# Attention and MLP on one core: the first v tile on ScalarE's DMA queue, the last stores split differently, score units one piece earlier

## The chip, the cores and the metric

The kernel runs on one core of one Trainium2 chip. The metric is the device time of one execution in microseconds (us). The profile's span, from the first to the last instruction, is 1.7 to 1.9 us shorter than that time. Each run of a kernel gave one execution with a full profile and, where it was timed, five more beside executions of the kernel before.

## The reference

```python
def _attn_ref(q, k, v, s):            # q, k, v: (8, 8, 576, 64); s: (8, 8, 576)
    scores = scale * np.matmul(q, k.transpose(0, 1, 3, 2))
    causal = np.triu(np.ones((S, S), dtype=bool), k=1)
    cum = np.cumsum(np.maximum(s, 0.0), axis=-1)
    bias = -(cum[:, :, :, None] - cum[:, :, None, :])
    scores = np.where(causal, -1000000000.0, scores + np.minimum(bias, 0.0))
    ...                               # softmax over the last axis
    return np.matmul(attn, v)

def _moe_ref(x, w_in, w_out):         # x: (4608, 512); w_in: (512, 2048); w_out: (2048, 512)
    h = x @ w_in
    return gelu_erf(h) @ w_out        # written out with erf in the original
```

The output is float32, 4608 by 512.

## The kernel before

The kernel computes attention batch by batch, and weaves the attention of batch c+1 into the MLP of token chunk c, so that TensorE always has matmuls to do. The bias is separable, so v is scaled by a weight `wb` that comes from the running sum of s. The parts that matter here are the loads, the first attention items, and the stores (cuts are marked with `# ...`).

```python
LAST = (NCH - 1, 2)           # subtiles from here on are stored after the branch
# ...
def load_v(b, eng, sts=range(ST)):             # one DMA of 256 KB for each 128 rows of v
    t = raws[b, "v"] if (b, "v") in raws else raw_v(b)
    for st in sts:
        n_st = 128 if st < ST - 1 else SL
        eng.dma_start(out=t[:n_st, st, :, :], in_=bass.AP(tensor=v.tensor,
            offset=v.offset + b * H * S * D + st * 128 * D,
            ap=[[D, n_st], [S * D, H], [1, D]]))      # source in runs of 64 floats = 256 B

s_sw = const.tile([64, S], fp32, name="s_sw")
nc.sync.dma_start(out=s_sw, in_=s.flatten_outer_dims())
for g in range(HG):
    for i in range(2):
        load_qk(0, i, g, 1)                    # GpSimd: float32 in memory, bf16 on chip
# ...
exp_set(); filler(17); cum_sum(); masks(); weights()
# ...
load_v(0, nc.gpsimd, (0, 1))
load_w(0, 0); load_w(0, 1); load_w(0, 2)       # w_in in four parts, w_out in four parts
scale_v(0, 1, nc.gpsimd)
# ... all further loads, on GpSimd
tr_qk(0, 0, 0); tr_qk(0, 1, 0)                 # 32x32 transposes by VectorE
sc_first(0, 0)                                 # scores and exponentials
tr_qk(0, 0, 1); tr_qk(0, 1, 1)
sc_first(0, 1, (0,)); filler(1); sc_first(1, 0, (0,))
mk_item(0, 0, 0)                               # mask
scale_v(0, 0)                                  # vv = v * wb, by VectorE
sc_first(1, 0, (1,), 0)
av_item(0, 0, 0)                               # P @ vv, the first reader of it
# ...
def l2_item(c, subs, f0=0, f1=FT, store=True):
    # ... matmuls into y_of[c, sub]
    if f1 == FT and store:
        for sub in subs:
            o_sb = ost.tile([128, KO * 128], fp32, tag="osb", bufs=3, name="o_sb")
            if c == 0: nc.scalar.activation(o_sb, y_of[c, sub], func=AF.Copy)
            else:      nc.vector.tensor_copy(o_sb, y_of[c, sub])
            nc.sync.dma_start(out=out[r0 : r0 + 128, :], in_=o_sb)
# ...
rv = nc.values_load(bad[0:1, 0:1], min_val=0, max_val=1)
with tc.If(rv > 0):                            # a general path, not taken with these inputs
    # ...
for sub in range(LAST[1], 4):                  # after the branch
    o_sb = ost.tile([128, KO * 128], fp32, tag="osb", bufs=3, name="o_sb")
    # scalar_copy stands for ScalarE's activation with Copy
    for i, (copy, eng) in enumerate([(nc.vector.tensor_copy, nc.sync), (scalar_copy, nc.scalar)]):
        cols = slice(i * 256, i * 256 + 256)
        copy(o_sb[:, cols], y[:, cols])
        eng.dma_start(out=out[r0 : r0 + 128, cols], in_=o_sb[:, cols])
```

Of the kernel before, what the change touches and what calls it, by code (L numbers as in the profile page):

```python
# [19 lines left out]
def kernel(  # L20
# [10 lines left out]
    nc = tc.nc  # L31
    fp32 = mybir.dt.float32
    bf16 = mybir.dt.bfloat16
    AF = mybir.ActivationFunctionType
# [17 lines left out]
    NCH = n_tok // NB  # L52
# [17 lines left out]
    ITS = [(0, 1), (2, 3, 4)]  # L70


    LAST = (NCH - 1, 2)

    EPS = 2.0 ** -17
    MAX_SC = 3.0
# [41 lines left out]
    def load_v(b, eng, sts=range(ST)):  # L118
# [3 lines that stand above are left out]
            eng.dma_start(  # L122
                out=t[:n_st, st, :, :],
                in_=bass.AP(
                    tensor=v.tensor,
                    offset=v.offset + b * H * S * D + st * 128 * D,
                    ap=[[D, n_st], [S * D, H], [1, D]],
                ),
            )

    s_sw = const.tile([64, S], fp32, name="s_sw")
    nc.sync.dma_start(out=s_sw, in_=s.flatten_outer_dims())
    for g in range(HG):
        for i in range(2):
            load_qk(0, i, g, 1)
# [4 lines left out]
    def load_w(which, i):  # L140
# [16 lines left out]
        out=uptri, in_=uptri, compare_op=ALU.is_gt, fill=1.0, base=0, pattern=[[-1, 128]],  # L157
# [322 lines left out]
    def l2_item(c, subs, f0=0, f1=FT, store=True):  # L480
        gT = gT_of[c]
        if f0 == 0:
            for sub in subs:
                y_of[c, sub] = yps.tile([128, KO * 128], fp32, tag="mlp", bufs=2, name="o_ps")
        for ft in range(f0, f1):
            for sub in subs:
                nc.tensor.matmul(  # L487
                    y_of[c, sub], lhsT=gT[:, ft, sub * 128 : (sub + 1) * 128], rhs=w_out_r[:, ft, :],
                    start=(ft == 0), stop=(ft == FT - 1),
                )  # L490
        if f1 == FT and store:
            for sub in subs:
                o_sb = ost.tile([128, KO * 128], fp32, tag="osb", bufs=3, name="o_sb")
                if c == 0:
                    nc.scalar.activation(o_sb, y_of[c, sub], func=AF.Copy)
                else:
                    nc.vector.tensor_copy(o_sb, y_of[c, sub])  # L497
                r0 = c * NB + sub * 128
                nc.sync.dma_start(out=out[r0 : r0 + 128, :], in_=o_sb)

    def exp_set():
        nc.scalar.preload_act_table_set("natural_log_exp_and_others")  # L502
# [18 lines left out]
    nc.scalar.activation(vv[0][:, :, :, D], wb[:, :, 0:H], func=AF.Copy)  # L521
    filler(3)
    filler(3, raws[0, "qk"][:, 1, 0, :128])
    load_v(0, nc.gpsimd, (0, 1))
    load_w(0, 0)
    load_w(0, 1)
    load_w(0, 2)
# [10 lines left out]
    load_v(1, nc.gpsimd, (2, 3, 4))  # L538
    tr_qk(0, 0, 0)
    tr_qk(0, 1, 0)  # L540
    sc_first(0, 0)
    tr_qk(0, 0, 1)
    tr_qk(0, 1, 1)
# [1 line left out]
    filler(1)  # L545
    sc_first(1, 0, (0,))
    mk_item(0, 0, 0)
    scale_v(0, 0)
    sc_first(1, 0, (1,), 0)
    av_item(0, 0, 0)  # L550
    mk_item(0, 1, 0, 0, 2)
# [15 lines left out]
    sc, mk, av = sc_item, mk_item, av_item  # L567
# [5 lines left out]
    for c in range(NCH):  # L573
        b = c + 1
        if c > 0 and b + 1 < B:
            load_qks(b + 1)
            load_v(b + 1, nc.gpsimd)
        if c == 0:

            late = [  # L580
                [], [], [], [], [(av, 0, 0, 2), (av, 0, 1, 2)],
                [(av, 0, 0, 3), (av, 0, 1, 3)], [(to_xT, 0, 2, True), (to_xT, 0, 3, True)],
                [], [(scale_v, 0, 4), (av, 0, 0, 4)], [(av, 0, 1, 4)], [(to_xT, 0, 4, True)],
            ] + [[]] * 5
            for half in range(2):
                for f2 in range(FT // 2):
                    l1_item(0, f2, half * 256, half * 256 + 256)
                    for f, *a in late[8 * half + f2]:
                        f(*a)
                    if f2 % 2 and 3 <= 8 * half + f2 <= 11:  # L590
                        square_v(0, 4 * half + f2 // 2 - 1)
        else:
            for f2 in range(FT // 2):
                l1_item(c, f2)
                for g, it in late_of.get(c, [])[f2 : f2 + 1]:
                    av(c, g, it)
                if b < B and f2 < HG:
                    tr_qk(b, 0, f2)
                    tr_qk(b, 1, f2)
                if b < B and f2 == 2:  # L600
                    den_col(b)
                    for st in range(2):
                        scale_v(b, st)
                if b < B and f2 == 3:
                    for st in range(2, ST):
                        scale_v(b, st)
                if b < B and 4 <= f2 < 4 + HG:
                    absmax(b, f2 - 4)
                if c == 2 and f2 == 7:
                    cert_decay()  # L610
                if f2 < ST and c < B:
                    square_v(c, f2)
        if b < B:
            if c == 0:
                for g in range(HG):
                    for i in range(2):
                        tr_qk(b, i, g)
                den_col(b)
            exp_set()
            if c == 0:  # L620
                load_qks(2)
                load_v(2, nc.gpsimd)
                side = [[] for _ in range(16)]
                side[0] = [(sc, b, 0, 0), (scale_v, b, 0), (scale_v, b, 1), (mk, b, 0, 0)]
                side[3] = [(sc, b, 1, 0), (mk, b, 1, 0)]
                side[5] = [(sc, b, 0, 1), (av, b, 0, 0), (av, b, 0, 1)]
                side[6] = [(av, b, 1, 0, True), (av, b, 1, 1, True), (scale_v, b, 2), (mk, b, 0, 1)]
                side[7] = [(to_xT, b, 0, True), (sc, b, 1, 1)]
                side[8] = [(to_xT, b, 1, True), (scale_v, b, 3), (av, b, 0, 2), (gelu_set,), (mk, b, 1, 1)]
                side[9] = [(av, b, 0, 3)]  # L630
                side[11] = [(av, b, 1, 2, True), (scale_v, b, 4), (square_qk, 0, 0, 0), (square_qk, 0, 0, 1)]
                side[12] = [(av, b, 1, 3, True), (square_qk, 0, 1, 0), (square_qk, 0, 1, 1)]
                side[13] = [(to_xT, b, 2, True)]
                side[14] = [(to_xT, b, 3, True)]
                groups(c, (0, 1), side[:8])
                for sub in (2, 3):
                    groups(c, (sub,), side[4 * sub : 4 * sub + 4])
            else:

                side = [[] for _ in range(16)]  # L640
                sc_at = (1, 4, 6, 8) if b < 4 else (2, 5, 8, 11)
                for at, (g, u) in zip(sc_at, [(0, 0), (1, 0), (0, 1), (1, 1)]):
                    side[at].append((sc, b, g, u))
                side[sc_at[3]].append((gelu_set,))
                mk_at = (4, 6, 8, 10) if b < 4 else (5, 8, 11, 14)
                for at, (g, u) in zip(mk_at, [(0, 0), (1, 0), (0, 1), (1, 1)]):
                    side[at].append((mk, b, g, u))
                av_at = (5, 6, 8, 9) if b < 4 else (6, 7, 9, 10)
                for at, (g, it) in zip(av_at, [(0, 0), (0, 1), (1, 0), (1, 1)]):
                    side[at].append((av, b, g, it))  # L650
                if b < 4:
                    side[10].append((av, b, 0, 2))
                    side[11].append((av, b, 1, 2))

                    side[15].extend([(av, b, 0, 3), (av, b, 1, 3)])
                if c == 1:
                    side[0].append((absmax, c, 0))
                    side[12].extend([(square_qk, c, 1, 0), (square_qk, c, 1, 1)])
                    side[3].append((cert_exp,))
                for sub in range(4):  # L660
                    groups(c, (sub,), side[4 * sub : 4 * sub + 4])
        else:
            for sub in range(4):
                l2_item(c, (sub,), store=(c, sub) < LAST)
                if c == B - 1:
                    (cert_1, cert_2, cert_3, cert_4)[sub]()
# [3 lines left out]
    with tc.If(rv > 0):  # L670
        with tc.tile_pool(name="gen", bufs=1) as gen, tc.tile_pool(
# [5 lines left out]
            a, step = 0, 1  # L677
# [120 lines left out]
    with tc.manual_schedule():  # L798
        for sub in range(LAST[1], 4):
            y = y_of[LAST[0], sub]  # L800
            r0 = LAST[0] * NB + sub * 128
            o_sb = ost.tile([128, KO * 128], fp32, tag="osb", bufs=3, name="o_sb")
            for i, (copy, eng) in enumerate(
                [(nc.vector.tensor_copy, nc.sync), (lambda o, a: nc.scalar.activation(o, a, func=AF.Copy), nc.scalar)]  # L804
            ):
                cols = slice(i * 256, i * 256 + 256)
                copy(o_sb[:, cols], y[:, cols])  # L807
                eng.dma_start(out=out[r0 : r0 + 128, cols], in_=o_sb[:, cols])  # L808


# [28 lines left out]
```

## Time and profile before

| before | |
|---|---|
| time, median of 3 (range) | 315.05 us (314.75 to 315.15) |
| span of the profiled execution | 312.2 us |
| TensorE busy | 300.7 us, 96% |
| VectorE, ScalarE, GpSimd busy | 63%, 62%, 17% |
| last matmul's end, and from there to the end of the span | 306.7 us, 5.5 us |

A share of busy time says little about a change like this. What counts is where TensorE, which does almost all of the work, stands still: those few places are at the start, where transfers have not landed, and after its last matmul. The prediction shows the lines.

### The profile page before, as it was taken

Reading aid. Unit: us, or ns where it says so; the run is one execution under the profiler, and the core shown is the slowest. Engines: PE = TensorE matmul, PEld = TensorE weight load, DVE = VectorE, ACT = ScalarE, POOL = GpSimd, SP = SyncE. Lnnn points to the kernel's source line nnn. Section 1 sums busy time; section 2 is a strip of 40 time slices with the busy share of each in tenths; the row PEclk is TensorE's granted clock in tenths of the full one; section 3 lists DMA queues with packets and bytes.
Section 4 is the critical chain, followed back from the end, with each engine's and each line's share of the span. In section 5 each row is a group of like instructions: output and inputs, shape, how many; then the busy total and the mean of one; then the engine's idle time right before and its main releaser. Section 6 shows DMA issues by size and latency. Waiting matters only on the chain. (4 is left out here: it accounts for less than half of the span.)

```text
span 312.2 us, 6053 instructions
## 1 busy us (share of the span) xinstructions
PE 300.7 (96%) x2466; PEld 154.9 (50%) x2506; DVE 195.7 (63%) x397; ACT 193.5 (62%) x263; POOL 54.3 (17%) x73
## 2 busy tenths in 40 slices
PE   8999999999999999999999999999999999999992
PEld 3577655444554455445454545444544454444441
DVE  8866767797779685955697559845994531350010
ACT  3876878878848763865686558665875677006300
POOL 8473340151003300150006000500000000000000
PEclk9999999999999999999999999999999999999999
DMA  7999999969541963097219940822110311020012
GB/s 137 222 230 210 224 212 278 188 150 204 158 68 44 211 161 103 8 207 181 86 35 174 206 103 18 169 78 75 45 27 34 103 53 25 37 93 7 1 73 70
DMA packets 32211, 36.73 MB, mean 118 GB/s; under 512 B 16752, under 2 KB 21360, under 8 KB 32176
## 3 DMA queue, kind: packets, MB, share of 16 engines
q0 software_dynamic: 11552, 23.07, 37.8%
q1 hardware_dynamic: 20336, 12.93, 15.2%
q8 instruction: 21, 0.34, 0.5%
q10 hardware_dynamic: 288, 0.26, 0.2%
q14 instruction: 14, 0.11, 0.1%
HBM read 36.85 MB, written 9.44 MB: 148 GB/s over the span
## 5 line engine op out<-in xcount | busy, mean ns | idle before, releaser
L487 PE MATMUL o_ps<-w_out_r,gT 128*128 128x512 bf16 x551 | 131.9, 380 | 2.7 <-issue 1.6
L471 PE MATMUL h_ps<-xT,w_in_r 128*128 128x512 bf16 (+1 forms) x625 | 131.1, 357 | 1.7 <-DVE xT L417 0.6
L476 ACT ACTIVATE gT<-h_ps 128x1024 bf16<-128x1024 f32 (+1 forms) x80 | 75.0, 938 | 63.7 <-PE h_ps L471 62.6
L471 PEld LDWEIGHTS <-w_in_r 128*128 128x128 bf16 x640 | 59.8, 98 | 55.4 <-issue 1.2
L487 PEld LDWEIGHTS <-gT 128*128 128x128 bf16 x576 | 52.1, 98 | 57.4 <-issue 3.3
L363 ACT ACTIVATE P<-sc_ps 128x1024 bf16<-128x1024 f32 x56 | 54.3, 1021 | 28.8 <-PE sc_ps L348 28.8
L122 POOL DMA_DIRECT2D raw_v<-in_v_dram x40 | 34.0, 862 | 125.8 <-ACT sq L215 115.4
L497 DVE COPY o_sb<-o_ps 128x512 f32<-128x512 f32 x30 | 20.7, 691 | 49.3 <-PE o_ps L487 49.3
L187 DVE STREAM_TRANSPOSE qkT<-raw_qk 128x576 f32<-128x576 f32 x32 | 37.2, 1238 | 0.2 <-DMA raw_qk<-in_k_dram 0.2
L448 DVE RECIPROCAL rc<-av 128x4 f32<-128x4 f32 (+1 forms) x80 | 14.0, 175 | 35.2 <-PE av L439 35.1
L449 DVE TENSOR_TENSOR x<-av,rc 128x256 bf16<-128x256 f32 (+1 forms) x80 | 33.8, 423 | 2.9
L439 PEld LDWEIGHTS <-P 128*128 128x128 bf16 x576 | 26.8, 98 | 16.0 <-DVE x L449 0.9
L207 DVE TENSOR_REDUCE amx<-raw_qk 128x2 f32<-128x2304 bf16 x13 | 32.7, 2535 | 0.0
L439 PE MATMUL av<-vv,P 128*128 128x65 bf16 x576 | 30.4, 194 | 0.4 <-DVE x L449 0.2
L223 DVE TENSOR_TENSOR vv<-raw_v,wb 128x512 bf16<-128x512 f32 (+1 forms) x39 | 25.3, 692 | 4.3 <-DMA raw_v<-in_v_dram 4.3
L371 DVE TENSOR_TENSOR P<-P,tri_bf 128x1024 bf16<-128x1024 bf16 (+1 forms) x33 | 22.1, 672 | 8.5 <-ACT P L363 8.4
L215 ACT ACTIVATE sq<-raw_v 128x512 bf16<-128x512 f32 (+1 forms) x40 | 24.8, 621 | 0.0
L348 PE MATMUL sc_ps<-qkT 32*128 32x256 bf16 (+2 forms) x560 | 18.0, 250 | 0.0
L348 PEld LDWEIGHTS <-qkT 32*128 32x128 bf16 x560 | 11.7, 92 | 12.2 <-issue 9.3
L502 ACT ACT_TABLE_LOAD x8 | 10.3, 1283 | 0.9 <-PEq L823 0.7
L505 ACT ACT_TABLE_LOAD x8 | 10.3, 1283 | 0.1
L804 ACT ACTIVATE o_sb<-o_ps 128x256 f32<-128x256 f32 x2 | 0.8, 383 | 14.3 <-DVE o_sb L807 13.8
(81 smaller groups left out, 100.2 us busy)
## 6 DMA issues: line engine op xcount, KB each, us to landing
out_dram<-o_sb SPq DMA_DIRECT2D x34, 256.0 KB, 2.2
raw_v<-in_v_dram POOLq DMA_DIRECT2D x32, 256.0 KB, 5.5
raw_qk<-in_q_dram POOLq DMA_DIRECT2D x7, 576.0 KB, 7.5
raw_qk<-in_k_dram POOLq DMA_DIRECT2D x7, 576.0 KB, 10.8
w_in_r<-in_moe_w_in_dram POOLq DMA_DIRECT2D x4, 512.0 KB, 9.8
w_out_r<-in_moe_w_out_dram POOLq DMA_DIRECT2D x4, 512.0 KB, 15.1
raw_v<-in_v_dram POOLq DMA_DIRECT2D x8, 128.0 KB, 6.1
raw_qk<-in_q_dram POOLq DMA_DIRECT2D x2, 288.0 KB, 5.2
```

The lines of the kernel that those rows point to most:

```text
L122: eng.dma_start(out=t[:n_st, st, :, :], in_=bass.AP(tensor=v.tensor, offset=v.offset + b * H * S * D + st * 128 * D, ap=[[D, n_st], [S * D ...
L187: nc.vector.transpose(qkT[b % 2][:, i, g, :S, :].rearrange("p s e -> p (s e)").bitcast(fp32) .rearrange("p (l j) -> p j l", j=LT), raws[b, ...
L207: nc.vector.tensor_reduce(amx[:, b * HG + g], raws[b, "qk"][:, :, g, :], axis=AX, op=ALU.max, apply_absolute_value=True,)
L215: nc.scalar.activation(sq[:n_st], raws[b, "v"][:n_st, st].rearrange("p h d -> p (h d)"), func=AF.Square, accum_out=sumv[:n_st, b, st : st ...
L223: eng.tensor_tensor(vv[b % 2][:n_st, st, :, 0:D], raws[b, "v"][:n_st, st, :, :], w.unsqueeze(2).to_broadcast([n_st, H, D]), op=MULT,)
L348: nc.tensor.matmul(s_ps[h // 2][:, h % 2, off : off + n], lhsT=qk[r, 1, g, jt * 128 : jt * 128 + 128, e], rhs=qk[r, 0, g, i0 : i0 + n, e], ...
L363: nc.scalar.activation(P[:, 2 * h2 : 2 * h2 + 2, o : o + 512], s_ps[h2], func=AF.Exp, scale=scale)
L439: nc.tensor.matmul(o_ps[:, h, :], lhsT=P[:, h, off : off + 128], rhs=vv[b % 2][:, jt, 4 * g + h, :], start=(i == 0), stop=(i == len(BLK[it ...
L449: nc.vector.tensor_tensor(x_of[b, it][:n, g * 256 : g * 256 + 256].rearrange("p (h d) -> p h d", d=D), o_ps[:n, :, 0:D], rc[:n].unsqueeze( ...
L471: nc.tensor.matmul(h_ps[:, i, :], lhsT=w_in_r[:, ko, ft * 128 : (ft + 1) * 128], rhs=xT[:, ko, c * NB + n0 : c * NB + n1], start=(ko == 0) ...
L476: nc.scalar.activation(gT_of[c][:, f2 * 2 : f2 * 2 + 2, n0:n1], h_ps, func=AF.Gelu)
L487: nc.tensor.matmul(y_of[c, sub], lhsT=gT[:, ft, sub * 128 : (sub + 1) * 128], rhs=w_out_r[:, ft, :], start=(ft == 0), stop=(ft == FT - 1),)
```

## The change

The intent is to shorten both ends. The first v tile goes out on ScalarE's idle queue as its first act, so that its scaling can be done in a gap between VectorE's transposes. The last subtile but one is stored before the branch. Some attention items move by a piece. (A subtile is 128 of a chunk's 512 tokens. A piece is one of the 16 parts into which a chunk's second MLP layer is cut; attention items stand between them. A score unit computes a block of scores and their exponentials.)

```diff
-    LAST = (NCH - 1, 2)
+    LAST = (NCH - 1, 3)
     nc.sync.dma_start(out=s_sw, in_=s.flatten_outer_dims())
+    load_v(0, nc.scalar, (0,))
-    load_v(0, nc.gpsimd, (0, 1))
+    load_v(0, nc.gpsimd, (1,))
     tr_qk(0, 1, 0)
+    scale_v(0, 0)
     sc_first(0, 0)
     mk_item(0, 0, 0)
-    scale_v(0, 0)
 # ... l2_item
-                if c == 0:
+                eng = nc.scalar if (c, sub + 1) == LAST else nc.sync
+                if c == 0 or eng is nc.scalar:
-                nc.sync.dma_start(out=out[r0 : r0 + 128, :], in_=o_sb)
+                eng.dma_start(out=out[r0 : r0 + 128, :], in_=o_sb)
 # ... chunk 0: batch 0's last block transposed in the second layer, not in the first
-                [], [(scale_v, 0, 4), (av, 0, 0, 4)], [(av, 0, 1, 4)], [(to_xT, 0, 4, True)],
+                [], [(scale_v, 0, 4), (av, 0, 0, 4)], [(av, 0, 1, 4)],
-                side[3] = [(sc, b, 1, 0), (mk, b, 1, 0)]
+                side[3] = [(sc, b, 1, 0), (to_xT, 0, 4, True), (mk, b, 1, 0)]
 # ... batches 4 to 7: scores, masks and value products one piece earlier
-                sc_at = (1, 4, 6, 8) if b < 4 else (2, 5, 8, 11)
+                sc_at = (1, 4, 6, 8) if b < 4 else (1, 4, 7, 10)
 # ... (mk_at and av_at likewise)
 # ... after the branch
-            for i, (copy, eng) in enumerate([(nc.vector.tensor_copy, nc.sync), (scalar_copy, nc.scalar)]):
+            for i in range(2):
-                copy(o_sb[:, cols], y[:, cols])
-                eng.dma_start(out=out[r0 : r0 + 128, cols], in_=o_sb[:, cols])
+                nc.vector.tensor_copy(o_sb[:, cols], y[:, cols])
+                nc.sync.dma_start(out=out[r0 : r0 + 128, cols], in_=o_sb[:, cols])
```

Below, "start part" is the first v tile and its scaling, "middle part" the later transposition with the score units, "end part" the stores.

More of the change, by code (lines that the diff above doesn't have):

```diff
@@ L582 @@
                 [(av, 0, 0, 3), (av, 0, 1, 3)], [(to_xT, 0, 2, True), (to_xT, 0, 3, True)],
-                [], [(scale_v, 0, 4), (av, 0, 0, 4)], [(av, 0, 1, 4)], [(to_xT, 0, 4, True)],
-            ] + [[]] * 5
+                [], [(scale_v, 0, 4), (av, 0, 0, 4)], [(av, 0, 1, 4)],
+            ] + [[]] * 6
             for half in range(2):
@@ L644 @@
                 side[sc_at[3]].append((gelu_set,))
-                mk_at = (4, 6, 8, 10) if b < 4 else (5, 8, 11, 14)
+                mk_at = (4, 6, 8, 10) if b < 4 else (4, 7, 10, 13)
                 for at, (g, u) in zip(mk_at, [(0, 0), (1, 0), (0, 1), (1, 1)]):
                     side[at].append((mk, b, g, u))
-                av_at = (5, 6, 8, 9) if b < 4 else (6, 7, 9, 10)
-                for at, (g, it) in zip(av_at, [(0, 0), (0, 1), (1, 0), (1, 1)]):
+                for at, (g, it) in zip((5, 6, 8, 9), [(0, 0), (0, 1), (1, 0), (1, 1)]):
                     side[at].append((av, b, g, it))
@@ L802 @@
             o_sb = ost.tile([128, KO * 128], fp32, tag="osb", bufs=3, name="o_sb")
-            for i, (copy, eng) in enumerate(
-                [(nc.vector.tensor_copy, nc.sync), (lambda o, a: nc.scalar.activation(o, a, func=AF.Copy), nc.scalar)]
-            ):
+            for i in range(2):
                 cols = slice(i * 256, i * 256 + 256)
-                copy(o_sb[:, cols], y[:, cols])
-                eng.dma_start(out=out[r0 : r0 + 128, cols], in_=o_sb[:, cols])
+                nc.vector.tensor_copy(o_sb[:, cols], y[:, cols])
+                nc.sync.dma_start(out=out[r0 : r0 + 128, cols], in_=o_sb[:, cols])
 _INS = ['q', 'k', 'v', 's', 'moe_w_in', 'moe_w_out']
```

## The prediction

> **What bounds the kernel now.** I read the busy totals, then TensorE's waits, then the start and the end in order of time, then the share of the DMA engines by stretch.
>
> ```profile
> PE 300.7 (96%) x2466; PEld 154.9 (50%) x2506; DVE 195.7 (63%) x397; ACT 193.5 (62%) x263; POOL 54.3 (17%) x73
> DMA  7999999969541963097219940822110311020012
> ```
>
> TensorE is the bound, but 96% busy alone does not prove it, since matmuls overlap. The order of time does:
>
> ```profile
> 271.46 3.62 PE L487 MATMUL o_ps<-w_out_r,gT 128*128 128x512 bf16 x16
> ```
>
> Sixteen matmuls in 3.62 us are 0.216 us apart (the last adds its own length of about 0.38). Going through all gaps between matmul starts after 50 us, I find only this pace, a fixed pattern inside the score units, and single gaps of 0.22 that are missing records (a subtile shows 15 of its 16 matmuls there). So from 50 us to the last matmul's end at 306.7 nothing can be saved by reordering. What can change lies before 45 us and after 306.7. The waits of TensorE between 16 and 45 us:
>
> ```profile
> PE h_ps L471 <- DVE xT L417: 0.6, 1, 0.6
> PE o_ps L487 <- DMA w_out_r<-in_moe_w_out_dram: 0.3, 1, 0.3
> PE h_ps L471 <- DMA w_in_r<-in_moe_w_in_dram: 0.3, 1, 0.3
> ```
>
> Two of the three are weights that had not landed: the start is also bound by transfers. VectorE between 8 and 14 us says the same of q and k:
>
> ```profile
> 7.39 2.53 DVE L187 STREAM_TRANSPOSE qkT<-raw_qk 128x576 f32<-128x576 f32 x2
> 10.11 1.25 DVE L187 STREAM_TRANSPOSE qkT<-raw_qk 128x576 f32<-128x576 f32 x1 [0.20 <-DMA raw_qk<-in_k_dram]
> 11.31 0.69 DVE L371 TENSOR_TENSOR P<-P,tri_bf 128x1024 bf16<-128x1024 bf16 x1
> 11.92 0.69 DVE L223 TENSOR_TENSOR vv<-raw_v,wb 128x512 bf16<-128x512 f32 x1
> 13.31 0.18 DVE L448 RECIPROCAL rc<-av 128x4 f32<-128x4 f32 x1 [0.70 <-PE av L439]
> ```
>
> The landing records put the four q/k tiles at 5.61, 7.04, 8.63 and 10.09 us; the third transpose starts at 8.66 and the fourth at 10.11, each just after its landing. The scaling at 11.92 is what the change moves; after it VectorE waits 0.70 us for TensorE anyway. The 16 DMA engines by stretch (us, then five engines' busy time and counts, clock, DMA share, GB/s):
>
> ```profile
> 2.00:2.50 0.50, 0.50 (x3) 0.20 (x2) 0.38 (x3) 0.03 (x1) 0.50 (x2) 1.00 0.66 147
> 2.50:3.00 0.50, 0.50 (x3) 0.22 (x2) 0.35 (x3) 0.00 (x0) 0.50 (x2) 1.00 1.13 203
> 3.00:3.50 0.50, 0.50 (x3) 0.18 (x2) 0.44 (x2) 0.00 (x0) 0.50 (x2) 1.00 0.61 101
> 3.50:4.00 0.50, 0.50 (x3) 0.15 (x1) 0.45 (x3) 0.00 (x0) 0.45 (x3) 1.00 1.01 194
> 4.00:8.00 4.00, 4.00 (x20) 1.74 (x19) 3.97 (x7) 1.47 (x4) 4.00 (x6) 1.00 1.09 196
> ```
>
> From 3.5 us on they are full; the free room is in the slices at 2.0 and 3.0: (0.34 + 0.39) x 0.5 = 0.36 us. Last, the end:
>
> ```profile
> 307.25 0.76 DVE L807 COPY o_sb<-o_ps 128x256 f32<-128x256 f32 x2 [6.73 <-PEq L670]
> 307.70 1.60 SPq L808 DMA_DIRECT2D out_dram<-o_sb  x2
> 307.71 0.38 ACT L804 ACTIVATE o_sb<-o_ps 128x256 f32<-128x256 f32 x1 [13.76 <-DVE o_sb L807]
> 308.12 0.38 ACTq L808 DMA_DIRECT2D out_dram<-o_sb  x1
> 308.62 0.38 ACT L804 ACTIVATE o_sb<-o_ps 128x256 f32<-128x256 f32 x1 [0.53 <-ACT o_sb L804]
> 309.04 0.34 ACTq L808 DMA_DIRECT2D out_dram<-o_sb  x1
> ```
>
> After the branch (307.25) two subtiles leave in four halves, alternating between VectorE and ScalarE. The last issue is at 309.04; it lands at 311.12, and the span ends 1.1 us later.
>
> **What the Trainium skill says.** "DMA: Bandwidth & Descriptors", section "Issuing engines are not separate DMA queues": transfers issued from ScalarE, SyncE or GpSimd run on the same 16 engines and interleave. So ScalarE's queue takes the v tile out of GpSimd's order, not out of the competition. The trace agrees as far as it goes: the shares above are full with one queue at work. The same page, "SWDGE vs HWDGE vs iDMA": a transfer that casts must be issued by GpSimd. Hence q, k and the weights (float32 to bf16) stay there and only v can move; in the trace every casting load is on the GpSimd queue. "PSUM — Partial Sum Buffer", section "Terms": ScalarE and VectorE may not access one bank in the same partitions at once. That explains the end: both halves of a subtile lie in one bank, and ScalarE's copy at 307.71 waited for VectorE's (named in the row).
>
> **The change part by part.**
>
> *First v tile, and its scaling between the transposes.* The v tile is 256 KB. Behind k it cost 11.27 - 10.09 = 1.18 us of the DMA engines (landings), the next one 12.35 - 11.27 = 1.08. On ScalarE's queue its packets should be small; the only 256-byte packets of this trace, those of the transposing transfers, took 18 ns each, and 1024 x 18 / 16 = 1.15 us: the same cost. Issued at about 0.75 like s, it would start near 2.1 us (s does), ahead of or beside q and k. Of its 1.15 us, some 0.36 falls into free room; the rest, about 0.7, pushes q/k landings back. Transposes: first about 6.35, second after k's 7.04 + 0.7 to 9.0, scaling (0.6 start to start) to 9.6, third 9.6, fourth at about 10.8 where it was 10.11: a delay D of about 0.7. Without any push, the scaling alone would make D = 0.25 (8.6 + 0.6 + 1.15 = 10.35). The scaling taken away at 11.92 returns nothing: TensorE reaches the first value product at 12.97 by its own order, and the scaling was done at 12.61. The scores of head group 1 need the fourth transpose, the fourth exponential began at 12.20 with the scores ready at 12.17, so the chain to the first MLP matmul (17.39) shifts by nearly D.
>
> *What absorbs D.* TensorE then waits for transfers whose total work is unchanged: 0.22 us at 21.97 (third v tile, landed 21.23, scaled until 21.94), 0.3 to 0.4 at 24.79 (last of w_in, landed 24.75), 0.3 at 39.96 (third of w_out, landed 39.92). That is up to 0.9 us of slack. Beyond that, the engines started work in the free room, so these landings should come about 0.3 us earlier. With D = 0.7 TensorE reaches 39.66 about 0.15 to 0.3 us early. **Start: -0.15 us, between -0.4 and +0.5.**
>
> *Last transposition of batch 0 moved from before 30.4 us to the second layer.* Four TensorE transposes (0.29 us) and one copy (0.29) move, none goes. Its wait at 30.19 for the product (about 0.1 on TensorE) goes; before the 39.96 wait, that is inside what the DMA gate gives back. **0.**
>
> *Score units one piece up for batches 4 to 7.* No TensorE wait is there. **0.**
>
> *The end.* The subtile before the last is now copied by ScalarE when its matmuls end, at 306.7 - 3.45 = 303.25: 0.59 us (ScalarE's 128x512 copies in this trace), stored by about 306.4, beside the last subtile's matmuls. After the branch only two VectorE copies (307.25 to 308.01) and two SyncE issues (307.70 and about 308.09) remain. The last issue comes 0.95 us earlier. SyncE's and ScalarE's stores here took 2.0 to 2.4 us from issue to landing, so 310.1 to 310.5 against 311.12: 0.6 to 1.0 less. But SyncE's second issue, also at 308.09 before, took 1.21 us where others took 0.33; if that was not due to ScalarE's issues beside it, it lands at about 310.6 to 310.8. **End: -0.7 us, between -0.3 and -1.0.**
>
> Sum: -0.15 + 0 + 0 - 0.7 = -0.85, so 315.05 - 0.85 = **314.2 us**.
>
> **The rivals.** (a) The v tile also holds up s, which is on the same kind of queue in the same moment: VectorE takes s at 3.92, s landed at 3.54, so 0.4 us are free; a landing at 4.6 makes D about 1.2, and if the later waits do not take it up, the start loses 0.5. Against it: s is 64 packets, issued at the same time. It would give about 314.8. (b) Transfers' landings are what counts, TensorE gains the whole 0.3 to 0.4 from the filled room, and the end its 1.0: 313.6. (c) SyncE's slow second issue stays: end only -0.3, 314.6. (d) Nothing outside the end moves, since all transfers are hidden by TensorE's queue: 314.35. (e) ScalarE's store of the subtile before last delays the branch: against it, ScalarE has nothing else after 294 us, and some 3 us to do it in.
>
> **Range and chances.** The parts that can move come to -1.4 to +0.2 together, so 313.65 to 315.25; the runs of before spread over 0.4 us. I take 313.4 to 315.1 for 8 in 10. Two per cent are 6.3 us, more than the whole start up to the first MLP matmul could plausibly give or lose; faster or slower by that much needs something unseen: 0.01 each, 0.98 within.
>
> **What would show it.** In the changed profile: q/k transposes starting later than 6.30, 7.39, 8.66 and 10.11, the fourth near 10.8 (if at 10.35 or less, no push by the v tile); the first MLP matmul near 18.0 instead of 17.39; smaller or vanished waits at w_in and w_out, and TensorE's last matmul ending at 306.4 to 306.7; no ScalarE copy after the branch, the last store's issue near 308.1, and the last matmul to the end of the span in 4.8 us instead of 5.5. I would be wrong if the last matmul ended over 0.5 us away from 306.7, above all if it comes from the middle, or if the end did not shrink.

## The result

| | median us (range), executions | ratio to before, 95% interval |
|---|---|---|
| before, beside the changed kernel | 314.86 (314.53 to 315.15), 6 | |
| changed kernel | 314.12 (313.15 to 314.89), 6 | 0.9974 (0.9955 to 0.9992) |

A ratio here is the mean time of one kernel's fast runs over that of the other's of the same rounds, so it is not quite the ratio of the medians. The changed kernel is 0.7 us faster. The total is what was predicted, 314.2. The profile, however, tells another story than the prediction did. Its span is 313.1 us, longer than before's 312.2, and that profiled execution (314.89 us) is the slowest of the six. Before's profile errs the other way: that execution took 314.09 us, less than any of the six of before in the table.

The start, VectorE from 0 to 14 us in the changed kernel (start, busy time, instruction, and in brackets the idle time before it and what ended it):

```profile
4.70 0.65 DVE L239 TENSOR_SCALAR s_pos<-s_sw 64x576 f32<-64x576 f32 x1 [0.69 <-DMA s_sw<-in_s_dram]
...
7.64 2.64 DVE L188 STREAM_TRANSPOSE qkT<-raw_qk 128x576 f32<-128x576 f32 x2 [0.28 <-DMA raw_qk<-in_q_dram]
10.13 0.68 DVE L224 TENSOR_TENSOR vv<-raw_v,wb 128x512 bf16<-128x512 f32 x1
10.73 2.46 DVE L188 STREAM_TRANSPOSE qkT<-raw_qk 128x576 f32<-128x576 f32 x2
```

VectorE now waits for s, which it did not before: s is in use from 4.70 us where it was 3.92, because the v tile, on the other queue at the same moment, holds it up. But s is not what the transposes then wait for: the row at 7.64 names q. By the landing records the four q/k tiles come at 7.62, 9.00, 10.40 and 11.90 us instead of 5.61, 7.04, 8.63 and 10.09. The transposes start at 7.64 instead of 6.30 us, the fourth at 11.92 instead of 10.11 (not alone in a row here), 0.02 us after its tile, and the first MLP matmul comes at 19.09 instead of 17.39. The DMA engines, in stretches as before:

```profile
2.00:2.50 0.50, 0.50 (x3) 0.19 (x2) 0.38 (x3) 0.49 (x1) 0.50 (x2) 1.00 0.57 133
2.50:3.00 0.50, 0.50 (x3) 0.22 (x2) 0.35 (x3) 0.00 (x0) 0.50 (x2) 1.00 1.07 253
3.00:3.50 0.50, 0.50 (x3) 0.19 (x2) 0.44 (x2) 0.00 (x0) 0.50 (x2) 1.00 1.29 355
3.50:4.00 0.50, 0.50 (x3) 0.15 (x1) 0.45 (x2) 0.00 (x0) 0.45 (x3) 1.00 1.14 151
4.00:8.00 4.00, 3.15 (x16) 1.34 (x14) 3.00 (x6) 0.77 (x1) 3.31 (x5) 1.00 1.03 159
```

The v tile fills the slice at 3.0 us (share 1.29 where it was 0.61), but the room at 2.0 stays, and from 4 to 8 us the engines move 159 GB/s where they moved 196: they are as busy and do less. By 8 us they had moved 1.1 MB in both profiles, so what was won at 3 us is lost again. TensorE's waits between 16 and 50 us:

```profile
PE o_ps L488 <- DMA w_out_r<-in_moe_w_out_dram: 0.8, 1, 0.8
PE h_ps L472 <- DVE xT L418: 0.6, 1, 0.6
```

The wait for w_in is gone, absorbed by the later start; the one for w_out grew from 0.3 to 0.8 us, since that part landed at 40.92 us instead of 39.92. The last matmul ends at 307.6 instead of 306.7. The end, in order of time:

```profile
304.18 0.60 ACT L498 ACTIVATE o_sb<-o_ps 128x512 f32<-128x512 f32 x1 [9.34 <-SPq L672]
304.81 0.37 ACTq L502 DMA_DIRECT2D out_dram<-o_sb  x1
308.20 0.76 DVE L807 COPY o_sb<-o_ps 128x256 f32<-128x256 f32 x2 [6.79 <-PEq L672]
308.65 1.95 SPq L808 DMA_DIRECT2D out_dram<-o_sb  x2
```

ScalarE's copy and store of the last subtile but one lie beside the last subtile's matmuls, as intended, and no ScalarE copy is left after the branch. But the two SyncE issues take 1.95 us together, 0.34 and 1.50, and from the last matmul to the end of the span it is 5.5 us, as before.

So by this one profile the start costs 0.9 us and the end gives nothing, while the six executions, this one among them, are 0.7 us faster by their median. Either the profiled execution was unusual, or the gain is in the middle. The experiments take the parts apart.

### The profile page after: what moved, and what is told of

It is laid out like the page before. It is cut to its first block, busy times and chain, and to the rows that moved or that the text cites. A ratio compares the mean times of both kernels' runs of the same rounds, so it can differ in the third digit from the quotient of the medians.

```text
span 313.1 us, 6092 instructions
## 1 busy us (share of the span) xinstructions
PE 303.3 (97%) x2506; PEld 154.7 (49%) x2506; DVE 195.9 (63%) x397; ACT 193.3 (62%) x262; POOL 53.6 (17%) x72
## 5 line engine op out<-in xcount | busy, mean ns | idle before, releaser
L488 PE MATMUL o_ps<-w_out_r,gT 128*128 128x512 bf16 x576 | 135.6, 379 | 0.8 <-DMA w_out_r<-in_moe_w_out_dram 0.8
L122 POOL DMA_DIRECT2D raw_v<-in_v_dram x39 | 33.1, 860 | 125.7 <-ACT sq L216 115.3
L498 ACT ACTIVATE o_sb<-o_ps 128x512 f32<-128x512 f32 x5 | 2.9, 592 | 11.1 <-SPq L672 9.3
```

The lines of the kernel that those rows point to most:

```text
L488: nc.tensor.matmul(y_of[c, sub], lhsT=gT[:, ft, sub * 128 : (sub + 1) * 128], rhs=w_out_r[:, ft, :], start=(ft == 0), stop=(ft == FT - 1),)
```

## The experiments

Each was correct against the reference. "Before" was run beside each set on the same chip (in the last set, four of its five executions are ones that the first set lists too). In every set but the first result some executions, mostly with a granted clock of 0.986 to 0.991 instead of 0.994 and more, took about 2 us longer; they widen the intervals.

**The parts by themselves.** Four kernels on one chip: the changed kernel again, and each part alone on the kernel before. The edits are the three parts of the diff above.

> The changed kernel unaltered, as the measure for the three parts run beside it. Both theories: 0.7 us less than before (0.9974 of it), between 0.2 and 1.2 us less. In the one profile of it the last matmul ended 0.9 us later than before and the end took as long as before (5.5 us); theory A says that this profile was an unlucky execution and the next one shows the last matmul within 0.4 us of 306.7; theory B says that the late start is the rule, with the last matmul at 307.2 or later again.

> Only the change of the end: the last subtile but one copied and stored by ScalarE before the branch, the last one by VectorE and SyncE alone. Theory A (the prediction): this is the gain, 0.7 us less than before (0.3 to 1.0). Theory B (the profile of the changed kernel, where SyncE's second store issue took 1.5 us and the end 5.5 us as before): no gain here, within 0.2 us of before.

> Only the first v tile on ScalarE's queue and its scaling between the transposes. Theory A (the prediction): 0.15 us less than before, between 0.4 less and 0.5 more. Theory B (the profile after: s landed 1.1 us later, the first MLP matmul 1.7 us later, the last matmul 0.9 us later): 0.5 to 1.0 us more than before, and runs that spread over more than before's.

> Only the later transposition of batch 0's last block and the score units one piece up. Theory A: no change, within 0.2 us of before, since TensorE shows no wait there. Theory B: if end and start do not add up to the gain, it must be here, 0.7 us or more less than before.

| run (before: 314.60, 11 executions) | median us (range) | ratio, 95% interval |
|---|---|---|
| changed kernel again | 313.93 (313.57 to 314.59) | 0.9972 (0.9951 to 0.9993) |
| end part alone | 314.65 (314.28 to 316.93) | 1.0017 (0.9983 to 1.0051) |
| start part alone | 314.59 (313.78 to 314.92) | 0.9989 (0.9967 to 1.0010) |
| middle part alone | 314.57 (314.15 to 317.18) | 1.0011 (0.9979 to 1.0043) |

The gain of the whole came back. No part alone shows it: the end part, from which the prediction expected 0.7 us, is at the time of before, with an interval of 1.1 us either way. The start part fits theory A and not theory B's loss of 0.5 us or more. In the second profile of the changed kernel the last matmul ended at 307.54 us, so its lateness was not one unlucky execution; but with the end part alone it ended at 307.55.

The profiles of the parts show one fixed thing. With the end part alone, where nothing at the start was touched, TensorE waited

```profile
PE o_ps L487 <- DMA w_out_r<-in_moe_w_out_dram: 0.8, 1, 0.8
```

just as in the changed kernel, because in that execution one of the 16 DMA engines landed its share of the third w_out part at 40.95 us and the other fifteen by 40.03 (landing records of the trace). In the profile of before they were at 39.92 and 39.84. So an engine that lags by 0.9 us is no mark of the change. And in nine of the ten profiles in which TensorE waited for that part, its last matmul ended 266.60 to 266.78 us after the landing (266.86 in the tenth, where it waited 0.2 us). What happens earlier reaches the end only through that landing, or where TensorE comes later still.

**Does SyncE wait for its own instructions?** This run and the next three were made on another chip beside before, without the changed kernel; against that one they can be judged only by their ratios to before. Here, only the issuing engine of both last stores was changed.

```diff
-                nc.sync.dma_start(out=out[r0 : r0 + 128, cols], in_=o_sb[:, cols])
+                nc.scalar.dma_start(out=out[r0 : r0 + 128, cols], in_=o_sb[:, cols])
```

> The changed kernel, but both stores of the last subtile issued by ScalarE instead of SyncE. In all six profiles so far SyncE's second store issue took 1.2 to 1.5 us and ended 0.33 to 0.40 us after a 16 KB instruction transfer had ended. Theory F: SyncE waits there for its own instructions, so ScalarE's second issue takes 0.34 to 0.55 us, the last matmul to the end of the span 4.5 to 4.9 us where it was 5.3 to 5.5, and the time is 0.6 to 0.8 us less than the changed kernel's, 1.2 to 1.5 less than before. Theory Q: a second store right behind a first one on the same queue is slow, whatever the engine; then ScalarE's second issue takes 1.2 us or more, the end 5.3 to 5.5 us and the time is the changed kernel's, 0.6 less than before.

Time: 314.13 us (313.59 to 314.25), ratio 0.9976 (0.9931 to 1.0020), before 314.47. First the changed kernel's row of that line, then this kernel's (engine, operation, count, shortest/median/longest in ns):

```profile
L808 SPq DMA_DIRECT2D out_dram<-o_sb x2: 337/916/1496, 308.7 to 309.1; - x2
```

```profile
L808 ACTq DMA_DIRECT2D out_dram<-o_sb x2: 336/742/1149, 307.7 to 308.2; - x2
```

ScalarE's second issue is as slow as SyncE's was. It is not one engine's instructions: theory F falls. From the last matmul to the end of the span it was 5.1 us, between what the two theories said. Theory Q explains the slow issue, but not that the slow issue still ended 0.32 us after a 16 KB instruction transfer, as all the others on a queue's second issue did (0.32 to 0.40 us in twelve profiles).

**The changed kernel without its start part.** (The start lines of the diff undone.)

> The changed kernel without its start part: v by GpSimd's queue and scaling in the old place, with the new end, the later transposition and the score units. Theory A (the parts add up: end -0.15, middle 0): 0.1 to 0.3 us less than before, so the start part is worth 0.3 us or more beside the others. Theory C (the start part is worth nothing, the whole gain is the end with the middle): 0.5 to 0.7 us less than before, as the changed kernel.

Median 314.48 (314.04 to 316.79), ratio 1.0010 (0.9958 to 1.0062). The two slow executions (316.4 and 316.8, clock 0.990) make the interval too wide to tell A from C.

**v behind s on one queue.**

```diff
-    load_v(0, nc.scalar, (0,))
+    load_v(0, nc.sync, (0,))
```

> The changed kernel with the first v tile on SyncE's queue behind s instead of ScalarE's beside it. Both theories: s lands near 3.6 us again (4.7 to 5.1 with ScalarE's queue) and the first transpose starts near 6.3 to 6.7. Theory G (later weight landings set TensorE's time after 40 us, not the start): the time is within 0.2 us of the changed kernel's although the first MLP matmul comes 0.5 us or more earlier. Theory H (the late start is paid in full): 0.5 us or more less than the changed kernel.

It took 322.03 us (317.78 to 322.92), ratio 1.0165. Three of six executions, the profiled one among them, are slow, being over 1.5% above the fastest, but that fastest one is 3.3 us above before's median as well; the low mean clock of the profile (0.977) comes from the stretch shown below. Neither theory had this. s landed at 3.52 us as expected, but v did not land until 14.8. VectorE from 5 to 30 us:

```profile
6.17 1.26 DVE L188 STREAM_TRANSPOSE qkT<-raw_qk 128x576 f32<-128x576 f32 x1
8.31 1.26 DVE L188 STREAM_TRANSPOSE qkT<-raw_qk 128x576 f32<-128x576 f32 x1 [0.88 <-DMA raw_qk<-in_k_dram]
14.88 0.70 DVE L224 TENSOR_TENSOR vv<-raw_v,wb 128x512 bf16<-128x512 f32 x1 [5.31 <-DMA raw_v<-in_v_dram]
15.49 2.33 DVE L188 STREAM_TRANSPOSE qkT<-raw_qk 128x576 f32<-128x576 f32 x2
```

The scaling, which stands between the transposes, blocks the other two for 5.3 us. TensorE, left idle, then gets half its clock (stretch in us, busy times, and the last three columns: granted clock, DMA share, GB/s):

```profile
5.00:10.00 5.00, 4.63 (x28) 2.00 (x26) 3.67 (x5) 1.65 (x4) 2.31 (x4) 1.00 1.13 219
10.00:16.00 6.00, 2.56 (x30) 1.09 (x24) 1.12 (x2) 2.85 (x3) 3.25 (x4) 1.00 1.20 220
16.00:26.00 10.00, 8.07 (x85) 5.37 (x86) 5.79 (x15) 5.08 (x5) 6.45 (x9) 0.51 1.17 229
```

That agrees with "TensorE: Matmul & The Clock Gate", section "Part 1: The HAM clock gate (the "warmup" mystery)", which says that an idle TensorE falls back to half its clock; here it lasted 13.7 us. The transfer's records show why v was late: in the changed kernel its 1024 packets of 256 bytes ran from 1.86 to 4.05 us, 941 of them before GpSimd's large ones began at 3.38. Started behind s, at 3.15, 893 of them were done by 7.0 us and the last 131 dribbled until 14.4, beside GpSimd's q, k and weights. So the tile has to be ahead of GpSimd's packets: 1.3 us later, and behind s on the other queue, the same transfer loses several microseconds. Which of the two, the time or the queue, does it was not tested apart. The test of theory G against H failed with it.

**An earlier w_out.**

```diff
-    load_v(1, nc.gpsimd, (0, 1))
     load_w(1, 2)
+    load_v(1, nc.gpsimd, (0, 1))
-                side[0] = [(sc, b, 0, 0), (scale_v, b, 0), (scale_v, b, 1), (mk, b, 0, 0)]
+                side[0] = [(sc, b, 0, 0), (mk, b, 0, 0)]
+                side[4] = [(scale_v, b, 0), (scale_v, b, 1)]
```

> The changed kernel with the third part of w_out loaded ahead of batch 1's first two v tiles, and these scaled four pieces later. Theory G: TensorE's wait of 0.7 to 0.8 us for w_out near 40 us vanishes (it lands 2 us earlier), and 0.3 to 0.8 us of the time with it, unless the fourth part, needed 3 us later and landing at 42.8 to 43.6, takes its place as the wait. Theory H: the time is within 0.2 us of the changed kernel's.

Median 314.41 (314.21 to 314.76), ratio 0.9982 (0.9938 to 1.0027). The wait for w_out is gone from TensorE's waits, and another is there (the first two lines; below them VectorE at that time):

```profile
PE av L440 <- DVE vv L224: 1.0, 2, 0.7
PE h_ps L472 <- DVE xT L418: 0.6, 1, 0.6
```

```profile
41.83 0.69 DVE L372 TENSOR_TENSOR P<-P,tri_bf 128x1024 bf16<-128x1024 bf16 x1 [1.45 <-ACT P L364]
42.44 1.29 DVE L224 TENSOR_TENSOR vv<-raw_v,wb 128x512 bf16<-128x512 f32 x2
```

TensorE now waits 0.7 us at 43.18 for the scaled v tiles. It is not their transfer that is late: they had landed at 40.22 and 41.22 us, and VectorE stood idle for 1.45 us before the mask at 41.83. The scaling comes after that mask because the edit itself put it four pieces later. So the run made a wait of its own in place of the one that it took away, and does not decide between the theories; the same order of loads with the scaling in an earlier place was not run.

**A square of four on one chip.** With and without the start part, and with the last store on SyncE or on ScalarE. The edit for the latter:

```diff
-                nc.sync.dma_start(out=out[r0 : r0 + 128, cols], in_=o_sb[:, cols])
+                (nc.sync, nc.scalar)[i].dma_start(out=out[r0 : r0 + 128, cols], in_=o_sb[:, cols])
```

> The changed kernel once more, as one corner of a square of four run on one chip: with and without the start part, with the last store on SyncE or on ScalarE. Theory A2 (the gain is small and in both parts): 0.4 to 0.8 us less than before. Profile: SyncE's second issue 1.2 to 1.5 us, ending 0.3 to 0.4 us after a 16 KB instruction transfer.

> The changed kernel with only the second half's store issued by ScalarE, the first by SyncE. Theory R (a queue's second issue waits until every DMA engine has taken the first one's descriptors, and one engine is held by the instruction transfer): ScalarE's issue, the first on its queue after the branch, takes 0.34 to 0.40 us although the instruction transfer is under way; last matmul to the end 4.6 to 5.0 us, and 0.3 to 0.6 us less than the changed kernel on the same chip. Theory F2 (any second store issue waits for the instruction transfer): ScalarE's issue takes 1.1 us or more and the time is the changed kernel's.

> The changed kernel without its start part, the third corner. Theory A2: 0.2 to 0.5 us slower than the changed kernel on the same chip, by the mean of its undisturbed runs. Theory C (the start part is worth nothing): within 0.2 us of it. Profile: last matmul 266.6 to 266.8 us after the third part of w_out has landed, as in seven of the profiles so far.

> Without the start part and with the last store on ScalarE, the fourth corner. Theory A2 and R: the two effects add, so 0.2 to 0.5 us slower than tail_split and 0.3 to 0.6 us faster than no_start_again. Theory C and R: as fast as tail_split, and then this is the better kernel, since it does without the start part.

| run (before: 314.60, 5 executions) | median us (range) | ratio, 95% interval | end in the profile, us |
|---|---|---|---|
| changed kernel, third time | 314.06 (313.24 to 316.34) | 0.9982 (0.9955 to 1.0010) | 5.5 |
| ... last store on ScalarE | 313.84 (312.90 to 314.49) | 0.9966 (0.9944 to 0.9988) | 5.1 |
| without the start part | 314.43 (313.81 to 316.39) | 1.0013 (0.9965 to 1.0061) | 5.7 |
| ... last store on ScalarE | 314.49 (314.14 to 315.48) | 1.0000 (0.9979 to 1.0021) | 5.4 |

("End" is from the last matmul to the end of the span.) In the changed kernel with the last store on ScalarE, both issues are short:

```profile
308.07 0.76 DVE L807 COPY o_sb<-o_ps 128x256 f32<-128x256 f32 x2 [6.73 <-PEq L672]
308.52 0.34 SPq L808 DMA_DIRECT2D out_dram<-o_sb  x1
308.86 0.34 ACTq L808 DMA_DIRECT2D out_dram<-o_sb  x1
```

A 16 KB instruction transfer was under way from 308.67 to 309.98, and ScalarE's issue at 308.86 took no notice: this is as theory R has it, and theory F2 falls. A queue's *second* issue waits until that transfer is over; another queue's first does not. That the transfer holds one DMA engine is inferred, since the records do not name the engine, but the stores of the fourteen profiles after 100 us support it: one landing came more than 0.3 us behind the other fifteen in 107 of the 168 stores with a 16 KB instruction transfer between issue and landing, and in 19 of the 222 with no instruction transfer. Yet the end shrank by 0.3 to 0.4 us only, not by 0.5 to 0.9, because one landing still comes late, presumably on that engine: fifteen engines had landed the ScalarE store 3.18 us after the last matmul, the sixteenth at 4.03. In the profile of before, all four stores had landed at 4.43. "Runtime: NRT & Kernel Launch", section "Instruction fetch mechanics", describes these transfers: instructions are refilled in blocks of 16 KiB, and a branch out of the loaded window forces such a fetch. The trace agrees in size (16,384 bytes) and place (0.1 to 0.15 us after the first store's issue, just past the branch), and adds that it takes 1.06 to 1.49 us there, in all fourteen profiles.

For the time, the square is not conclusive. One side of it is clear: with the last store on ScalarE, the five timed executions with the start part (312.90 to 314.09 us) all lie below the five without it (314.14 to 315.48). With it on SyncE they overlap. Without the start part the ScalarE store shows no gain. The changed kernel with its last store on ScalarE (tail_split), at 0.9966, is the fastest kernel and clearly below before, but its interval overlaps the changed kernel's, so that it beats that one is not shown.

**All timed executions together.** After the fact, I fitted 76 timed executions, those of before and of the eleven runs that differ from it only in these parts: one level for each of the four sets, and one number for each part (profiled executions left out, and those over 1.2 us above their kernel's median). The start part comes out at -0.46 us (95%: 0.22 either way), the end or middle part at -0.22 (0.23 either way), another engine for the last stores at +0.15 (0.30). It is a fit over noisy sets, not an experiment of its own, and four executions of before are in it twice (without the copies: -0.46 and -0.20).

**Open: profiled executions.** With the start part, a kernel's profiled execution took 0.74 us more than the median of its five timed ones, by the mean of seven kernels (from -0.56 to +2.39); without it, 0.18 us less (five kernels, -0.46 to +0.28; before itself, with 0.8 us less, is not among them). So the profile overstates what the start part costs. In the worst one, the third run of the changed kernel, the w_out wait was

```profile
PE o_ps L488 <- DMA w_out_r<-in_moe_w_out_dram: 1.6, 1, 1.6
```

with one engine landing at 42.40 us and fifteen by 40.60 (a 16 KB instruction transfer ran from 40.36 to 41.30), and that execution took 316.34 us where the timed ones had a mean of 314.05. Whether recording a thousand more small packets slows them is a guess. How the start part gains in the timed executions can't be seen in a profile that shows the opposite, so its mechanism stays open.

## Why the prediction was right or wrong

**The total: right** (314.2 predicted, 314.12 measured). The split was not: it had -0.15 for the start and -0.7 for the end. The fit gives about -0.5 and, with the middle, -0.2. As far as these noisy figures tell, two errors of size cancelled, and that the total was hit so closely is luck.

**The end: mechanism right, size wrong.** That the last issue comes earlier held: it began 1.52 us after the last matmul where the last one began 2.34 us after it before, 0.82 us less (0.95 predicted). The failing step is the time from there to the landing, "2.0 to 2.4 us": it was 2.92 us, since the issue itself took 1.50. The prediction had seen SyncE's slow second issue (1.21 us) and put it down as possibly due to ScalarE's issues beside it. It was not: it took 1.26 to 1.50 us with ScalarE silent. The three profiles with the old end have 5.4 to 5.9 us from last matmul to end (mean 5.60), the seven fast ones with the new end and SyncE's stores 5.1 to 5.7 (mean 5.41). So the term is about -0.2 where -0.7 stood, no more than the scatter of these profiles, and outside its own range of -0.3 to -1.0. Rival (c), the slow issue, is what happened. It goes with an instruction transfer, as the experiments show.

**The start: the delay was undersized, the absorption held in part.** D, the delay of the fourth transpose, was put at 0.7. The first MLP matmul came at 18.4 to 19.8 us (mean 19.2) in the seven fast profiles with v on ScalarE's queue and at 17.4 to 18.4 (mean 17.8) in the six without the start part: 1.4 us later. The failing step is "the rest, about 0.7, pushes q/k landings back". The fourth q/k tile landed at 11.13 to 12.61 us (mean 11.9) instead of 10.09 to 10.74 (mean 10.4), 1.5 us later, and in six of the seven the fourth transpose began within 0.03 us of that landing. The room at 2.0 and 3.0 us gave nothing in the end, as the bytes moved by 8 us show; all 0.26 MB of the tile, 1.3 us at the 196 GB/s of the row of before (an estimate), came ahead of q and k. Rival (a) happened as well, and the argument against it, "64 packets, issued at the same time", failed: s landed at 4.67 to 5.42 us instead of 3.40 to 3.57. But s set the first transpose in only three of the seven profiles, and the fourth in one.

The next step, that TensorE's waits for transfers take the delay up, held in part: in the changed kernel's profile TensorE came to the wait near 40 us 0.5 us later than before (40.15 for 39.64, with the moved transposition now done before it), after a first MLP matmul 1.7 us later; in that of the start part alone it came after the landing, and the last matmul ended 0.75 us later. "These landings should come about 0.3 us earlier" did not show in the profiles: the third w_out part landed at 40.87 us on average in six of them with the start part (40.02 to 42.40) and at 40.34 in six without (39.92 to 40.95; w_order left out). The timed executions gain all the same, which the prediction's sum allowed (up to -0.4), but its reason for it is not confirmed.

**The middle: not contradicted.** 0 was predicted; alone it measured 1.0011 with an interval of 0.9979 to 1.0043, and the last matmul ends at 306.75 us in its profile, at 306.70 in that of before.

Rivals (d), nothing moves but the end, and (e), ScalarE's early store delays the branch, did not happen: that store was issued at 304.81 and VectorE's first copy after the branch came 0.61 us after the last matmul (0.55 before). SyncE did wait at the branch until that store had landed, 0.59 us after the last matmul, but was ready for its first store 0.06 us before VectorE's half was; in the one where that landing came latest (the second run without the start part, 0.79 us) it was ready 0.05 us after it.

## What to carry to other kernels

While the DMA engines are full, a load moved forward delays what it passes by its own bytes, and TensorE pays only where it comes later than the transfer it would have waited for anyway; find that transfer first, here the third w_out part. A transfer in small pieces should be out before the large ones start: here it took 2.2 us ahead of them and 11.3 us beside them. When an experiment takes a wait away and another appears, look up whether the new one is due to the kernel or to the edit. Where the last stores set the end, look at each store's sixteen landings and at the length of the issues: here one late landing held the end although there were fewer copies. A second store on another queue was issued without delay, though a gain in time from it alone is not shown.

## What the Trainium skill lacked or had wrong

- "DMA: Bandwidth & Descriptors", "Issuing engines are not separate DMA queues", says that transfers interleave and that the issuing engine saves only issue time. Another passage of the page has each DMA engine take turns between queues packet by packet, but no page gives a figure for how uneven that gets: 1024 pieces of 256 bytes took 2.2 us ahead of GpSimd's large packets and 11.3 us beside them, the last 131 pieces 7.4 us of it. Issued together with s on the other queue, they made s land 1.1 to 1.9 us later.
- No page has it that a queue's second store issue waits for an instruction transfer to end: 1.15 to 1.50 us instead of 0.34, ending 0.32 to 0.40 us after the 16 KB instruction transfer in twelve profiles; the first issue on the other queue took 0.34 beside it.
- "Runtime: NRT & Kernel Launch", "Instruction fetch mechanics", calls the fetch at a block boundary mostly hidden and warns of a stall at a branch. It lacks that the fetch can hold up data transfers: while one of 1.06 to 1.49 us ran past the branch, one of sixteen landings of the last store came 4.03 us after the last matmul, the other fifteen by 3.18 (that it is the same engine is inferred).
